# A fused layernorm + MLP on one Trainium2 core: tiles 4 to 7 transposed by DMA, tile 0 in two halves, and a reordered last group

## The chip, the cores and the metric

The kernel runs on one core of a Trainium2 chip (trn2). The time is the device time of one execution in microseconds (us). The profile's span, from the first to the last instruction, is about 2 us shorter than the time. PE is TensorE, PEld its weight loads, DVE is VectorE, ACT ScalarE, POOL GpSimd, SP SyncE (here the engine that issues nearly all DMAs).

## The reference

```python
B, S, D, F = 1, 2048, 1024, 3584          # all inputs bfloat16

def reference(x, w1, b1, w2, b2):
    y = _layernorm(x, axis=-1)             # eps 1e-5, no scale or shift
    h = gelu_tanh(einsum("bsd,df->bsf", y, w1) + b1)
    return einsum("bsf,fd->bsd", h, w2) + b2
```

## The kernel before

Both matrix products use a seven-product scheme (Strassen in Winograd's form), on sums of quarters of the operands. The sums are made on DVE. The 16 row tiles of x (128 rows each) form two blocks of 8. Each tile is normalized, and must be transposed before it can be the moving operand: `to_yT_pe` does this on PE and copies the result out of PSUM on ACT; `to_yT_dma` does it by DMA. Before, all 8 tiles of block 0 went through PE and the 8 of block 1 through DMA.

The program is not written in its final order. Each `op` and `dma` records a task with an estimated duration. A list scheduler orders the tasks of each engine, and a randomized packing places every buffer in SBUF. When two buffers share bytes, the later one's first write waits for the earlier one's last reader. So an edit anywhere moves the order and *deals the placement anew*.

The parts that the change and the argument touch:

```python
def norm(i):                              # DVE, one row tile
    for h in range(2):
        op("DVE", 0.62, ... bn_stats ...)                # statistics of half h
    op("DVE", 0.25, ... bn_aggr ...); op("DVE", 0.1, ... + eps ...)
    op("POOL", 0.5, ... pow -0.5 ...)                    # rstd
    op("DVE", 0.47, ... (x - mean) * rstd ...)           # all 1024 columns
...
def to_yT_pe(b, i, bank):                 # 8 transposes into one PSUM bank, two ACT copies out
    def f(e):
        for k in range(KD):
            r = e.transpose(out=pv[:, k, :], in_=v16(xbuf, k * 256, 256), identity=ident[:, :])
        return r
    op("PE", KD * MM128, f, ...)
    for h in range(2):
        op("ACT", A_CP, ... copy of half h ...)
...
def tsum(b, t):                           # T sums of tiles t and t + 4, on DVE
    T1 = B12 - B11;  T2 = B22 - T1;  B12 = B22 - B12 (T3);  T4 = B21 - T2
```

```python
# head: "wave" = products of 128 columns, tile by tile, 7 weight rows each
for t in range(4):
    wave(t, range(0, 4))
    if t < 3: to_yT_pe(0, t + 1, 7)
    else:     b1_transpose(7)
    wave(t, range(4, WAVE_ROWS))
...
# then full-width products (512 columns); tiles 4 to 7 are transposed among them
for r in range(RH):
    ...p1(r + 1)...; p2(r)
    if nt < 8 and r in HEAD_T:            # HEAD_T = (2, 4, 6, 7)
        to_yT_pe(0, nt, 7); tsum(0, nt - 4); nt += 1
warm(1, bank=7, full=True)
# from here on the products need T1..T4 of block 0: "the first T product" is T2's
...
flat += [(last, 7), (last, 4), (last, 3)]  # the last group's last three products
```

```python
# Wino.step, one group of seven products in four PSUM banks X, Y, Z, Wb
elif q == 7:
    self.prod(7, Y, False)
    s3 = save(Y, n + "s3", mem=MA)        # ACT copies bank Y to SBUF
    add(Z, Z, s3, n + "V")                # DVE
    self.sink["22"](Z)                    # DVE add, store
elif q == 4:
    self.prod(4, Y, False)                # adds to bank Y: waits for the copy
    self.sink["21"](Y)
```

## Time and profile before

| | before |
|---|---|
| time, median of the first 3 runs (range) | 340.43 us (340.21 to 341.08) |
| span of the profiled run | 338.0 us |
| PE busy | 331.9 us, 98% of the span, granted clock 1.00 |
| DVE busy | 295.3 us, 87% |
| first full-width product | 17.02 us |
| first T product | 32.12 us |

PE's own waits come first. Each line says who waited, for whom, and then the total in us, how often, and the longest:

```profile
PE ps L1145 <- POOL nhalf L605: 1.0, 1, 1.0
PE ps L871 <- DVE mem L751: 0.8, 1, 0.8
PE ps L1124 <- ACT mem L806: 0.7, 1, 0.7
PE ps L1175 <- ACT mem L690: 0.2, 1, 0.2
PE ps L871 <- ACT ps L797: 0.2, 1, 0.2
```

In 338 us PE shows 2.9 us of waits (the other 3.1 us without work come after its last matmul, which ends at 334.88 us). Of this, 1.0 is the start, where nothing can run yet. The 0.7 us of L1124 lies in the last group: product 4 waits for ACT's copy of bank Y.

Next is the timeline of PE in the head, in order of time. The columns are start, duration, engine, line, operation, tiles, and the count of merged instructions; in brackets stand the idle time before and what ended it:

```profile
7.35 0.62 PE L685 MATMUL ps<-ident,mem 128*128 128x128 f16 x8
...
8.65 1.07 PE L1175 MATMUL ps<-mem 128*128 128x128 f16 x16 [0.23 <-ACT mem L690]
...
10.00 1.91 PE L1175 MATMUL ps<-mem 128*128 128x128 f16 x28
...
17.02 2.75 PE L871 MATMUL ps<-mem 128*128 128x512 f16 x12
19.61 0.61 PE L685 MATMUL ps<-ident,mem 128*128 128x128 f16 x8
```

L685 are transposes and L1175 is the wave. Transposes stand between the wave's parts, and from 17.02 us on between the full-width products (L871) as well: 4 times 8 of them, 0.45 us each.

The middle, same view, from the filler product L1145 on:

```profile
31.91 0.38 PE L1145 MATMUL ps<-ones 128*128 128x512 bf16 x1
32.12 47.79 PE L871 MATMUL ps<-mem 128*128 128x512 f16 x220
...
86.39 3.84 PE L871 MATMUL ps<-mem 128*128 128x512 f16 x17 [0.82 <-DVE mem L751]
```

The first T product starts at 32.12 us. The start of the piece at 86.39 us is the 305th full-width matmul of the program. I call it **M**.

The table by stretch shows for three stretches (us) the busy time of each engine (count of instructions), the granted clock, the DMA share and the traffic:

```profile
core 0: us, PE busy (x) PEld busy (x) DVE busy (x) ACT busy (x) POOL busy (x), PEclk, DMA share, GB/s
48.00:60.00 12.00, 12.00 (x58) 5.42 (x56) 11.83 (x23) 11.49 (x22) 2.31 (x3) 1.00 1.13 338
60.00:72.00 12.00, 12.00 (x57) 5.45 (x56) 11.56 (x23) 11.88 (x23) 5.26 (x5) 1.00 1.12 345
72.00:87.00 15.00, 13.98 (x63) 5.66 (x62) 15.00 (x33) 10.23 (x18) 0.76 (x2) 1.00 1.17 301
```

PE, DVE and the DMA engines are all full here. And the traffic in the 40 slices of the span, from the page (8.45 us each):

```profile
GB/s 233 324 193 7 281 268 345 356 287 335 284 300 320 287 304 357 308 338 323 312 32 218 109 235 96 184 147 143 225 165 180 175 116 230 170 169 249 204 103 63
```

The fourth slice, from 25 to 34 us, moves next to nothing: this is the room for the DMA transposes.

The end of the kernel, timeline of all engines (weight loads and DMA issues left out):

```profile
331.01 0.58 ACT L806 COPY mem<-ps 128x512 f32<-128x512 f32 x1 [2.47 <-PE ps L1124]
...
331.65 3.23 PE L1124 MATMUL ps<-mem 128*128 128x256 f16 x28 [0.68 <-ACT mem L806]
...
333.39 0.69 DVE L1056 TENSOR_TENSOR mem<-ps,mem 128x512 bf16<-128x512 f32 x1 [0.34 <-PE ps L1124]
334.92 0.69 DVE L1056 TENSOR_TENSOR mem<-ps,mem 128x512 bf16<-128x512 f32 x1 [0.84 <-PE ps L1124]
```

L806 is the copy that product 4 waits for; the last 28 matmuls are products 4 and 3, and each then needs a 512-column finish on DVE (L1056).

### The profile page before, as it was taken

Reading aid. Unit: us, or ns where it says so; the run is one execution under the profiler, and the core shown is the slowest. Engines: PE = TensorE matmul, PEld = TensorE weight load, DVE = VectorE, ACT = ScalarE, POOL = GpSimd, SP = SyncE. Lnnn points to the kernel's source line nnn. Section 1 sums busy time; section 2 is a strip of 40 time slices with the busy share of each in tenths; the row PEclk is TensorE's granted clock in tenths of the full one; section 3 lists DMA queues with packets and bytes.
Section 4 is the critical chain, followed back from the end, with each engine's and each line's share of the span. In section 5 each row is a group of like instructions: output and inputs, shape, how many; then the busy total and the mean of one; then the engine's idle time right before and its main releaser. Section 6 shows DMA issues by size and latency. Waiting matters only on the chain.

```text
span 338.0 us, 6056 instructions
## 1 busy us (share of the span) xinstructions
PE 331.9 (98%) x2363; PEld 222.0 (66%) x2363; DVE 295.3 (87%) x481; ACT 179.4 (53%) x311; POOL 15.2 (5%) x28
## 2 busy tenths in 40 slices
PE   8999999999999999999999999999999999999995
PEld 6854444443344444444446888888888888888884
DVE  5698899999999869967978992799999999999844
ACT  2699899996667676766765545534111222222110
POOL 2210110230000000000000000000000000000000
DMA  7970899999999999999917382644756537558732
GB/s 233 324 193 7 281 268 345 356 287 335 284 300 320 287 304 357 308 338 323 312 32 218 109 235 96 184 147 143 225 165 180 175 116 230 170 169 249 204 103 63
DMA packets 99382, 75.83 MB, mean 224 GB/s; under 512 B 12186, under 2 KB 90650, under 8 KB 99354
## 3 DMA queue, kind: packets, MB, share of 16 engines
q1 hardware_dynamic: 99210, 75.32, 74.6%
q8 instruction: 18, 0.29, 0.4%
q10 hardware_dynamic: 144, 0.13, 0.1%
q14 instruction: 10, 0.08, 0.1%
HBM read 48.96 MB, written 24.38 MB: 217 GB/s over the span
## 4 chain that ended last, share of the span: by engine, by line
PE 85%; DVE 9%; DMA 2%; issue 2%; POOL 0%; ACT 0%; DVEq 0%
PE ps L1124 44%; PE ps L871 37%; DVE ps L814 2%; PE ps L1175 2%; DVE mem L751 2%; DVE mem L937 2%; DVE st_sb L656 2%; DMA mem<-in_w_dram 1%; PE ps L685 1%; DMA mem<-in_x_dram 1%; DVE mem L717 1%; POOL rstd_sb L662 0%; DVE mem L664 0%; DVE mem L1056 0%; DVE mem L651 0%
## 5 line engine op out<-in xcount | busy, mean ns | idle before, releaser
L871 PE MATMUL ps<-mem 128*128 128x512 f16 x756 | 165.4, 379 | 1.0 <-DVE mem L751 0.8
L1124 PE MATMUL ps<-mem 128*128 128x256 f16 (+1 forms) x1372 | 150.6, 273 | 0.7 <-ACT mem L806 0.7
L1124 PEld LDWEIGHTS ps<-mem 128*128 128x128 f16 x1372 | 134.1, 98 | 17.5 <-ACT mem L806 1.0
L871 PEld LDWEIGHTS ps<-mem 128*128 128x128 f16 (+1 forms) x756 | 73.2, 98 | 89.8 <-DVE mem L751 2.2
L806 ACT COPY mem<-ps 128x512 f32<-128x512 f32 x111 | 65.0, 593 | 82.3 <-PE ps L1124 67.3
L790 ACT ACTIVATE mem<-ps,b_sb 128x512 f16<-128x512 f32 x112 | 73.3, 696 | 26.1 <-PE ps L871 15.6
L814 DVE TENSOR_TENSOR ps<-ps,mem 128x512 f32<-128x512 f32 x84 | 58.3, 695 | 23.8 <-ACT mem L806 21.8
L1028 DVE TENSOR_TENSOR mem<-mem 128x1792 f16<-128x1792 f16 x56 | 59.7, 1083 | 4.2 <-PE ps L1124 4.2
L751 DVE TENSOR_TENSOR mem<-mem 128x1024 f16<-128x1024 bf16 (+1 forms) x56 | 37.5, 685 | 0.6 <-DMA mem<-in_w_dram 0.2
L937 DVE TENSOR_TENSOR mem<-mem 128x512 f16<-128x512 f16 (+5 forms) x84 | 37.4, 463 | 0.7 <-DMA mem<-in_w_dram 0.4
L1039 DVE TENSOR_TENSOR mem<-mem 128x1792 f16<-128x1792 f16 x32 | 33.4, 1084 | 0.4 <-PE ps L871 0.4
L797 ACT COPY ps<-ps 128x512 f32<-128x512 f32 x31 | 17.7, 572 | 26.5 <-PE ps L1124 20.4
L656 DVE BATCH_NORM_STATS2 st_sb<-mem 128x6 f32<-128x512 bf16 x24 | 15.6, 675 | 6.0 <-DMA mem<-in_x_dram 5.9
L1056 DVE TENSOR_TENSOR mem<-ps,mem 128x512 bf16<-128x512 f32 x24 | 16.3, 686 | 3.5 <-PE ps L1124 3.5
L921 DVE TENSOR_TENSOR mem<-mem 128x2048 f16<-128x2048 bf16 (+1 forms) x16 | 17.3, 1083 | 0.0
L1069 DVE TENSOR_TENSOR mem<-ps,mem 128x512 f32<-128x512 f32 x24 | 16.2, 682 | 0.0
L690 ACT COPY mem<-ps 128x512 f16<-128x512 f16 x16 | 8.7, 603 | 8.9 <-PE ps L685 8.9
L717 DVE TENSOR_TENSOR mem<-mem 128x512 f16<-128x512 f16 x32 | 12.2, 418 | 0.1
L662 POOL TENSOR_TENSOR rstd_sb<-vpe_sb,nhalf 128x1 f32<-128x1 f32 x12 | 7.9, 663 | 50.2 <-DVE vpe_sb L659 50.2
L1145 PE MATMUL ps<-ones 128*128 128x128 bf16 (+1 forms) x58 | 7.3, 297 | 1.0 <-POOL nhalf L605 1.0
L1175 PE MATMUL ps<-mem 128*128 128x128 f16 x112 | 7.6, 219 | 0.3 <-ACT mem L690 0.2
L664 DVE TENSOR_SCALAR mem<-mem,mv_sb,rstd_sb 128x1024 f16<-128x1024 bf16 x12 | 6.3, 536 | 0.8 <-POOL rstd_sb L662 0.7
(30 smaller groups left out, 66.5 us busy)
## 6 DMA issues: line engine op xcount, KB each, us to landing
mem<-in_w_dram SPq DMA_DIRECT2D x80, 256.0 KB, 5.0
mem<-w_scr SPq DMA_DIRECT2D x28, 448.0 KB, 3.5
w_scr<-mem SPq DMA_DIRECT2D x21, 512.0 KB, 5.2
w_raw<-mem SPq DMA_DIRECT2D x12, 512.0 KB, 5.5
mem<-w_raw SPq DMA_DIRECT2D x12, 448.0 KB, 4.3
out_dram<-mem SPq DMA_DIRECT2D x32, 128.0 KB, 2.8
mem<-in_w_dram SPq DMA_DIRECT2D x9, 448.0 KB, 4.5
mem<-in_x_dram SPq DMA_DIRECT2D x15, 256.0 KB, 4.6
```

Of the source, the lines that this page charges most:

```text
L656: op("DVE", 0.62, lambda e, i=i, h=h: e.bn_stats(st_sb[:, i, 6 * h:6 * (h + 1)], v16(b, h * D, D, BF16)), r=[b.c(h)], w=[c_st[i][h]], name ...
L751: op("DVE", d_tt(n), lambda e: e.tensor_tensor(out=o[0], in0=a[0], in1=bb[0], op=f), r=[a[1], bb[1]], w=[o[1]], name=f"w1S{k}_{ch}")
L790: op("ACT", A_GELU, lambda e: e.activation(out=dst, in_=bank2(bank), func=ACT.Gelu_apprx_tanh, bias=b1_sb[:, f:f + 1], scale=1.0), r=[bank ...
L797: op("ACT", A_CP, lambda e: e.copy(out=banks[dst][:, :], in_=banks[src][:, :]), r=[bank_c[src]], w=[bank_c[dst]], name=name, lat=A_LAT)
L806: op("ACT", A_CP, lambda e: e.copy(out=v16(a, 0, 2048, F32), in_=banks[src][:, :]), r=[bank_c[src]], w=[a.c()], name=name, lat=A_LAT)
L814: op("DVE", D_PS, lambda e: e.tensor_tensor(out=banks[dst][:, :], in0=banks[src][:, :], in1=v16(a, 0, 2048, F32), op=ALU.add), r=[bank_c[s ...
L871: i = e.matmul(banks[bank][:, :], lhsT=lv[:, k, :], rhs=rv[:, k, :], start=(fresh and k == 0), stop=(k == KH - 1), skip_group_check=True)
L921: op("DVE", d_tt(2 * self.n), lambda e: e.tensor_tensor(out=vd, in0=va, in1=vb, op=ALU.subtract), r=self.cells(a) + self.cells(bb), w=self ...
L937: tt = lambda o, a, c: (lambda e: e.tensor_tensor(out=o, in0=a, in1=c, op=ALU.subtract))
L1028: op("DVE", d_tt(UN // 2), lambda e: e.tensor_tensor(out=v16(t), in0=a[0], in1=bb[0], op=f), r=a[1] + bb[1], w=[t.c()], name=f"in{b}_{p}{q}")
L1039: op("DVE", d_tt(UN // 2), lambda e, va=va, vb=vb, vd=vd: e.tensor_tensor(out=vd, in0=va, in1=vb, op=f), r=h_cells(b, a, u, s) + h_cells(b ...
L1124: i = e.matmul(bank2(bank)[:, t, :], lhsT=av3[:, k, t * P:(t + 1) * P], rhs=bv[:, k, :], start=(fresh and t == 0 and k == 0), stop=(t == 1 ...
```

## The change

The intent is to take work out of PE's stream at three places. At the head, PE shall start earlier, on half a normalized tile, and the seven weight rows of each wave tile stand 3 + 4 around the next tile's transposes instead of 4 + 3. In the middle, DMA shall transpose tiles 4 to 7, in a time when it is idle. At the end, product 3 shall hide the copy that product 4 waits for, and product 4 shall come in two halves in two fresh banks, so that the finish of the first overlaps the second. The rest tunes the scheduler to this: a look-ahead of 0.3 us (HOLD), another assumed start of PE, another packing seed, and more lead for the w2 units.

```diff
+HOLD = 0.3
-HEAD_T = (2, 4, 6, 7)
-UNIT_LA, IN_LA = (4, 5), 5
+UNIT_LA, IN_LA = (6, 5), 5
-T_PE = 7.5
-SEED = 2
+T_PE = 6.0
+SEED = 6
+HEAD_DUE = (6.0, 2.0)
...   scheduler: an engine may wait up to HOLD for a more urgent task; packing: more starts
-                op("DVE", 0.47, lambda e: e.tensor_scalar(out=v16(b), ...
+                for o, n in ((0, D * 2),) if i else ((0, D), (D, D)):
+                    op("DVE", 0.47 if i else 0.27, lambda e, o=o, n=n: e.tensor_scalar(
...
-            to_yT_pe(0, 0, 7)
-            warm(8, bank=6)
+            to_yT_pe(0, 0, 7, 6)          # half 0 into bank 7, half 1 into bank 6
+            warm(5, bank=5)
...
-                wave(t, range(0, 4))
+                wave(t, range(0, 3))
...
-                wave(t, range(4, WAVE_ROWS))
+                wave(t, range(3, WAVE_ROWS))
...
-            nt = 4
+            for i in range(4, 8):
+                due(lambda: (to_yT_dma(0, i), tsum(0, i - 4)), HEAD_DUE[0] + HEAD_DUE[1] * (i - 4))()
             for r in range(RH):
...
-                if nt < 8 and r in HEAD_T:
-                    to_yT_pe(0, nt, 7)
-                    tsum(0, nt - 4)
-                    nt += 1
...
-            flat += [(last, 7), (last, 4), (last, 3)]
+            flat += [(last, 7), (last, 3), (last, 4)]
...
+                    elif q == 4 and self.last:
+                        self.sink["21"](Y, (self.prod, self.s3, (X, (X + 4) % 8)))
...
+                        elif p == 3 and end is not None:
+                            prod, s3, fresh = end
+                            e6 = E.pop(("6", k))
+                            op("DVE", D_PS, ... e6 += s3 ...)
+                            for t in range(2):
+                                prod(4, fresh[t], True, t)
+                                finish(b, 0, 1, u, v, banks[fresh[t]][:, :], ..., t, 1, ("ACTQ", "SP")[t])
```

More of the change, by code (lines that the diff above doesn't have):

```diff
@@ L200, in pack @@
         weight = {i: self.size[i] * (self.gone[i] - self.born[i]) for i in ids}
-        order = sorted(ids, key=lambda i: -weight[i])
-        for tries in range(400):
+        for tries in range(600):
+            if tries % 100 == 0:
+                order = sorted(ids, key=lambda i: -weight[i] * (rng.uniform(0.7, 1.3) if tries else 1.0))
             self.off[:] = -1
@@ L385, in _simulate @@
                             break
-                        _, _, t = heapq.heappop(heaps[e])
+                        t = heaps[e][0][2]
+                        if HOLD and any(r < now + HOLD and w.alap < min(t.alap - 0.05, now + 4.0) and r < now + t.dur for r, _, w in waiting[e]):
+                            break
+                        heapq.heappop(heaps[e])
                     t.start = now
@@ L663, in norm @@
                    r=[c_vpe[i], c_nh], w=[c_rstd[i]], name=f"rstd{i}", lat=0.2)
-                op("DVE", 0.47, lambda e: e.tensor_scalar(out=v16(b), in0=v16(b, 0, D * 2, BF16), scalar1=mv_sb[:, i, 0:1],
-                                                          scalar2=rstd_sb[:, i:i + 1], op0=ALU.subtract, op1=ALU.mult),
-                   r=[c_mv[i], c_rstd[i]], w=[b.c(0), b.c(1)], name=f"norm{i}")
+                for o, n in ((0, D * 2),) if i else ((0, D), (D, D)):
+                    op("DVE", 0.47 if i else 0.27, lambda e, o=o, n=n: e.tensor_scalar(
+                        out=v16(b, o, n), in0=v16(b, o, n, BF16), scalar1=mv_sb[:, i, 0:1], scalar2=rstd_sb[:, i:i + 1],
+                        op0=ALU.subtract, op1=ALU.mult),
+                       r=[c_mv[i], c_rstd[i]], w=[b.c(h) for h in range(2) if o <= h * D < o + n], name=f"norm{i}")
             y = {}
@@ L675, in yv, with to_yT_pe, tr, f @@
                 return v3(y[b, c], 0, KD * CT * 2, KD)
-            def to_yT_pe(b, i, bank):
+            def to_yT_pe(b, i, bank, other=None):
                 c, t = (i % 8) // 4, i % 4
                 xbuf = xb[i]
-                pv = banks[bank][:, :].bitcast(F16).rearrange("p (k s) -> p k s", k=KD)
-                def f(e):
-                    for k in range(KD):
-                        r = e.transpose(out=pv[:, k, :], in_=v16(xbuf, k * 256, 256), identity=ident[:, :])
-                    return r
-                op("PE", KD * MM128, f, r=[xbuf.c(0), xbuf.c(1), c_id], w=[bank_c[bank]], name=f"T{i}", lat=PE_LAT)
+                pv = [banks[z][:, :].bitcast(F16).rearrange("p (k s) -> p k s", k=KD) for z in (bank, bank if other is None else other)]
+                cell = [bank_c[bank], bank_c[bank if other is None else other]]
+                def tr(ks):
+                    def f(e):
+                        for k in ks:
+                            r = e.transpose(out=pv[k // KH][:, k, :], in_=v16(xbuf, k * 256, 256), identity=ident[:, :])
+                        return r
+                    return f
+                if other is None:
+                    op("PE", KD * MM128, tr(range(KD)), r=[xbuf.c(0), xbuf.c(1), c_id], w=[cell[0]], name=f"T{i}", lat=PE_LAT)
+                else:
+                    for h in range(2):
+                        op("PE", KH * MM128, tr(range(h * KH, (h + 1) * KH)), r=[xbuf.c(h), c_id], w=[cell[h]], name=f"T{i}_{h}", lat=PE_LAT)
                 yy = yv(b, c)
@@ L690, in to_yT_pe @@
                     op("ACT", A_CP, lambda e, h=h: e.copy(out=yy[:, h * KH:(h + 1) * KH, t * P:(t + 1) * P],
-                                                         in_=pv[:, h * KH:(h + 1) * KH, :]),
-                       r=[bank_c[bank]], w=[y[b, c].c((h, t))], name=f"Te{i}_{h}", lat=A_LAT)
+                                                         in_=pv[h][:, h * KH:(h + 1) * KH, :]),
+                       r=[cell[h]], w=[y[b, c].c((h, t))], name=f"Te{i}_{h}", lat=A_LAT)
                 M.free(xbuf)
@@ L822, in __init__ @@
                     self.X, self.Y, self.Z, self.Wb = (4 * bset + k for k in range(4))
-                    self.s1 = None
+                    self.s1, self.last = None, False
                     self.done = set()
@@ L856, in step @@
                         add(Z, Z, s3, n + "V")
-                        MA.free(s3)
+                        if self.last:
+                            self.s3 = s3
+                        else:
+                            MA.free(s3)
                         self.sink["22"](Z)
+                    elif q == 4 and self.last:
+                        self.sink["21"](Y, (self.prod, self.s3, (X, (X + 4) % 8)))
+                        MA.free(self.s3)
                     elif q == 4:
@@ L1043, in out_sum, with store, finish @@
                         H[b, nm, s] = H.pop((b, place, s))
-            def store(b, i, k, u, v, o):
-                tb = b * TB + i * 512 + u * 256
+            def store(b, i, k, u, v, o, t0=0, nt=2, q="SP"):
+                tb = b * TB + i * 512 + u * 256 + t0 * P
                 c0 = k * 512 + v * NCOL
-                dma("SP", lambda e: e.dma_start(of[tb:tb + 256, c0:c0 + NCOL].rearrange("(t p) c -> p t c", p=P),
-                                                v16(o, 0, 1024, BF16).rearrange("p (t c) -> p t c", t=2)),
-                    [o.c()], [], P * 1024, None, f"st{b}{i}{k}{u}{v}")
+                dma(q, lambda e: e.dma_start(of[tb:tb + nt * P, c0:c0 + NCOL].rearrange("(t p) c -> p t c", p=P),
+                                                v16(o, 0, nt * 512, BF16).rearrange("p (t c) -> p t c", t=nt)),
+                    [o.c()], [], P * nt * 512, None, f"st{b}{i}{k}{u}{v}")
                 M.free(o)
-            def finish(b, i, k, u, v, a, na, bb, nb, name):
-                o = M.alloc(1024, "o")
-                op("DVE", D_PS, lambda e: e.tensor_tensor(out=v16(o, 0, 1024, BF16), in0=a, in1=bb, op=ALU.add),
+            def finish(b, i, k, u, v, a, na, bb, nb, name, t0=0, nt=2, q="SP"):
+                o = M.alloc(nt * 512, "o")
+                n = nt * NCOL
+                a, bb = a[:, t0 * NCOL:t0 * NCOL + n], bb[:, t0 * NCOL:t0 * NCOL + n]
+                op("DVE", 0.08 + n / 960, lambda e: e.tensor_tensor(out=v16(o, 0, 2 * n, BF16), in0=a, in1=bb, op=ALU.add),
                    r=[na, nb], w=[o.c()], name=name, lat=D_PS_LAT)
-                store(b, i, k, u, v, o)
+                store(b, i, k, u, v, o, t0, nt, q)
             E = {}
@@ L1070, in addto, with f @@
                            r=[bank_c[bank], src.c()], w=[dst.c()], name=name, lat=D_PS_LAT)
-                    def f(bank):
+                    def f(bank, end=None):
                         k = (b, u, v)
@@ L1095, in f @@
                             addto(e6, bank, e6, n)
+                        elif p == 3 and end is not None:
+                            prod, s3, fresh = end
+                            e6 = E.pop(("6", k))
+                            op("DVE", D_PS, lambda e: e.tensor_tensor(out=av(e6), in0=av(e6), in1=av(s3), op=ALU.add),
+                               r=[e6.c(), s3.c()], w=[e6.c()], name=n + "s3", lat=D_PS_LAT)
+                            for t in range(2):
+                                prod(4, fresh[t], True, t)
+                                finish(b, 0, 1, u, v, banks[fresh[t]][:, :], bank_c[fresh[t]], av(e6), e6.c(), f"{n}_{t}", t, 1,
+                                       ("ACTQ", "SP")[t])
+                            M.free(e6)
                         elif p == 3:
                             e6 = E.pop(("6", k))
-                            finish(b, 0, 1, u, v, banks[bank][:, :], bank_c[bank], av(e6), e6.c(), n)
+                            finish(b, 0, 1, u, v, banks[bank][:, :], bank_c[bank], av(e6), e6.c(), n, q="ACTQ" if (b, u) == (NB - 1, 1) else "SP")
                             M.free(e6)
@@ L1114, in prod2, with f @@
             def prod2(b, p):
-                def f(q, bank, fresh):
+                def f(q, bank, fresh, t=None):
                     av_, ac = a_unit(b, p, q)
@@ L1119, in f @@
                     bf = UNITS[p, q]
+                    ts = range(2) if t is None else (t,)
                     def g(e):
-                        for t in range(2):
+                        for t in ts:
                             for k in range(KQ):
                                 i = e.matmul(bank2(bank)[:, t, :], lhsT=av3[:, k, t * P:(t + 1) * P], rhs=bv[:, k, :],
-                                             start=(fresh and t == 0 and k == 0), stop=(t == 1 and k == KQ - 1), skip_group_check=True)
+                                             start=(fresh and t == ts[0] and k == 0), stop=(t == ts[-1] and k == KQ - 1), skip_group_check=True)
                         return i
-                    op("PE", 2 * KQ * MM256, g, r=ac + [bf.c()] + ([] if fresh else [bank_c[bank]]), w=[bank_c[bank]],
+                    op("PE", len(ts) * KQ * MM256, g, r=ac + [bf.c()] + ([] if fresh else [bank_c[bank]]), w=[bank_c[bank]],
                        name=f"m2_{b}_{p}{q}", lat=PE_LAT)
-                    if b == NB - 1:
-                        M.free(UNITS.pop((p, q)))
-                    ina_drop(b, p, q)
+                    if t != 0:
+                        if b == NB - 1:
+                            M.free(UNITS.pop((p, q)))
+                        ina_drop(b, p, q)
                 return f
@@ L1147, in warm, with due, g @@
                 op("PE", n * (MM512 if full else MM128), f, r=[c_ones] + ([gate] if gate is not None else []), w=[bank_c[bank]], name="warm")
+            def due(f, after):
+                def g():
+                    pr.due = (pr.last_pe, after)
+                    f()
+                    pr.due = None
+                return g
             y_new(0, 0)
@@ L1220, in build @@
                 p2(r)
-                if nt < 8 and r in HEAD_T:
-                    to_yT_pe(0, nt, 7)
-                    tsum(0, nt - 4)
-                    nt += 1
-            assert nt == 8
             warm(1, bank=7, full=True)
@@ L1277, in build @@
             fC = first_use(c_seq[0], (1,))
-            def due(f, after):
-                def g():
-                    pr.due = (pr.last_pe, after)
-                    f()
-                    pr.due = None
-                return g
             y1at = Y1_AT
@@ L1351, in build @@
                 n_g += 1
-            import os
+            groups[last].last = True
             for i, (g, q) in enumerate(flat):
```

## The prediction

> **What bounds the kernel.** TensorE. The page has PE busy 331.9 of 338.0 us at full clock, and the chain of waits is 85% PE. PE's own wait list is short: 1.0 us at the start, 0.7 before the last 28 matmuls (on the ACT copy L806), 0.8 at 85.6 us (on DVE's weight sum L751), 0.2 and 0.2. VectorE is a close second: the windows show it busy 11.8 of 12, 11.6 of 12 and 15.0 of 15 us between 48 and 87 us, and the chain runs through it from 52.6 to 86.4 us. Only work taken out of PE's stream, or out of the ends, counts, and DVE may take it back.
>
> **What changes, costed from the trace.**
> 1. *Head.* Before, the norm of tile 0 starts at 6.75, its 8 transposes at 7.35, the ACT copy at 8.01, the first wave matmul at 8.65. With halves the first transposes need half a norm (about 0.28 instead of 0.48 us), and only 4 transposes (0.22 of 0.45 us) come before the copy. The order shows one more statistics instruction ahead, costing about 0.1 us. Gain about 0.4 us. Weights (landing 6.8, 7.7, 8.5, 10.1 us) and x tile 3 (9.3 us) are just early enough.
> 2. *Middle.* Four PE transposes at 0.45 us leave: 1.8 us. With the head, PE would want the first T product at about 30.0 instead of 32.3 us. But the four DMA transposes are issued behind the weight loads, from about 20.4 us on, at 1.2 to 2.6 us each, and landed 2.5 to 3.5 us after issue in the trace; tile 7 should land at 29 to 30 us. DMA was idle here (7 GB/s in the fourth slice). The Trainium skill, "Advanced Engine Details and Errata", section X-Bar Transpose, says such transposes are as fast as regular DMAs; the trace agrees on packets alone (1024 of 256 bytes in 1.0 us when queued behind others, 2.4 us when not), not on issue. DVE is tighter still: from 20.7 us it has two norms, six weight sums (0.6 us pitch) and fourteen T sums (0.335) until the last tile's T2, ready at about 30.7. So PE will probably wait 0.5 to 1 us before the first T product. Net about 1.0 us.
> 3. *DVE-bound stretch to 87 us.* The order shows nearly the same DVE work ahead of each chunk's sums; its idle 2.4 us around 33 to 36 us shrinks, so the shift passes on. The waits of 1.0 us at 80 and 86 us change by some tenths at most.
> 4. *Tail.* Product 3 now stands between 7 and 4, and 4 goes into fresh banks: the 0.68 us PE wait goes. One more DVE add (about 0.6 us) comes in; the last add is 256 instead of 512 wide (about 0.4 of 0.69 us). DVE ends the kernel: V add, s3 add, two full finishes, two halves, done about 3.9 us after product 7, against 4.6 before. The last store (1.84 us to landing) hardly shortens. Gain about 0.7 us.
>
> **Sum.** About 0.4 + 1.0 + 0.2 + 0.7 = 2.3 us: **338.0 us**, range 336.3 to 339.6. Faster by over 2% (below 333.6) 2%, within 2% 97%, slower 1%.
>
> **What would show it.** First wave matmul at 8.2 to 8.3; no transposes in PE after tile 3; a PE wait before the first T product at 29.8 to 31 us, put down to DVE T sums or a transposing DMA; PE busy about 330; no gap before the last 28 matmuls; DVE back to back at the end.
>
> **What would make it wrong.** Transposes landing after 31 us (a stall eats the 1.8 us); landing before 28 with DVE ahead (gain to 3.5 us); new waits on weight units or buffers from the other packing; DVE falling behind between 48 and 87 us.

## The result, and the profile after

| | before | after |
|---|---|---|
| time, median (range) of 4 runs each | 340.32 us (339.98 to 341.08) | 338.19 us (337.74 to 338.62) |
| span of the profiled run | 338.0 us | 336.0 us |
| PE busy | 331.9 us | 329.9 us |
| DVE busy | 295.3 us | 298.3 us |

The ratio is 0.9934, with a 95% interval of 0.9910 to 0.9958: faster by 0.4 to 0.9%, clear of noise, but small. Ratios here and below are the mean time of one kernel's runs over that of the other's of the same rounds, so not quite the ratio of the medians that I quote.

PE's waits after:

```profile
PE ps L1180 <- POOL nhalf L610: 1.0, 1, 1.0
PE ps L891 <- DVE mem L731: 0.8, 1, 0.8
PE ps L891 <- ACT ps L811: 0.4, 1, 0.4
PE ps L891 <- DVE mem L765: 0.4, 1, 0.4
PE ps L1217 <- DMA mem<-in_w_dram: 0.2, 1, 0.2
PE ps L891 <- ACT mem L804: 0.2, 1, 0.2
```

The wait in the last group (0.7 us on ACT) is gone. New is 0.8 us on DVE L731: that line is the T sums.

PE in the head (L1217 is the wave, L891 the full-width products):

```profile
8.57 0.84 PE L1217 MATMUL ps<-mem 128*128 128x128 f16 x12
...
9.70 0.83 PE L1217 MATMUL ps<-mem 128*128 128x128 f16 x12
10.74 1.05 PE L1217 MATMUL ps<-mem 128*128 128x128 f16 x16 [0.20 <-DMA mem<-in_w_dram]
...
12.07 1.73 PE L1217 MATMUL ps<-mem 128*128 128x128 f16 x28
...
16.76 13.11 PE L891 MATMUL ps<-mem 128*128 128x512 f16 x60
...
30.87 5.35 PE L891 MATMUL ps<-mem 128*128 128x512 f16 x24 [0.78 <-DVE mem L731]
```

The first wave matmul starts at 8.57 us, only 0.08 us earlier than before. DVE's norm of tile 0 tells why. Before (L664, whole) and after (L670, two halves):

```profile
6.75 0.55 DVE L664 TENSOR_SCALAR mem<-mem,mv_sb,rstd_sb 128x1024 f16<-128x1024 bf16 x1
7.04 0.72 DVE L670 TENSOR_SCALAR mem<-mem,mv_sb,rstd_sb 128x512 f16<-128x512 bf16 x2
```

From there to the first wave matmul it takes 1.53 us instead of 1.90, but the norm starts 0.29 us later. On the other hand, 28 wave matmuls now take 1.73 us instead of 1.91. At 10.74 us PE waits 0.20 us for the weights of the wave's last row. The full-width products start at 16.76 instead of 17.02 us, and run through without transposes. The first T product comes at 30.87 us, after 0.78 us of waiting. The transposes on SP's queue, and the T sums on DVE in the same time, are these:

```profile
20.04 7.05 SPq L713 DMA_TRANSPOSE mem<-mem  x4
```

```profile
25.53 5.95 DVE L731 TENSOR_TENSOR mem<-mem 128x512 f16<-128x512 f16 x16 [0.16 <-DMA mem<-mem]
31.40 1.41 DVE L765 TENSOR_TENSOR mem<-mem 128x1024 f16<-128x1024 f16 x2
```

The trace has the four transposes landing at 25.50, 26.35, 27.76 and 28.96 us. The 16 T sums then run back to back. The 14th, T2 of the last pair of tiles, ends at 30.81 us, and PE goes on at 30.87 us.

The rest of PE's waits, and the same stretches as before:

```profile
75.84 2.76 PE L891 MATMUL ps<-mem 128*128 128x512 f16 x12 [0.42 <-DVE mem L765]
78.78 6.34 PE L891 MATMUL ps<-mem 128*128 128x512 f16 x28 [0.17 <-ACT mem L804]
85.54 4.71 PE L891 MATMUL ps<-mem 128*128 128x512 f16 x21 [0.42 <-ACT ps L811]
```

```profile
48.00:60.00 12.00, 12.00 (x57) 5.38 (x56) 11.45 (x22) 11.40 (x21) 1.92 (x3) 1.00 1.17 315
60.00:72.00 12.00, 11.97 (x56) 5.25 (x55) 11.93 (x24) 11.87 (x22) 2.49 (x3) 1.00 1.05 322
72.00:87.00 15.00, 13.99 (x63) 5.55 (x61) 14.86 (x34) 10.69 (x19) 1.67 (x3) 1.00 1.15 296
```

M is at 85.54 us. The end:

```profile
329.28 3.77 PE L1158 MATMUL ps<-mem 128*128 128x256 f16 x33
...
330.02 0.58 ACT L820 COPY mem<-ps 128x512 f32<-128x512 f32 x1 [2.47 <-PE ps L1158]
330.64 0.70 DVE L828 TENSOR_TENSOR ps<-ps,mem 128x512 f32<-128x512 f32 x1 [1.46 <-ACT mem L820]
331.25 0.68 DVE L1121 TENSOR_TENSOR mem<-mem 128x512 f32<-128x512 f32 x1
331.85 1.94 DVE L1078 TENSOR_TENSOR mem<-ps,mem 128x512 bf16<-128x512 f32 x4
```

PE runs through all the last products (L1158, 33 in the piece) and DVE ends the kernel: V add, the new add of s3 (L1121), two full finishes and two halves in one piece (L1078 x4).

The span's 1.96 us divide by PE's marks as follows. In each trace all 756 full-width matmuls and all 1372 of the output stage are recorded.

| stretch | before | after | gain, us |
|---|---|---|---|
| start to first full-width product | 17.02 | 16.76 | 0.26 |
| to the first T product | 15.10 | 14.11 | 0.99 |
| to the first output-stage matmul (181.49, 180.51 us) | 149.37 | 149.64 | -0.27 |
| to the end of the span | 156.47 | 155.49 | 0.98 |

### The profile page after: what moved, and what is told of

Read it like the earlier page. It is cut to its first block, busy times and chain, and to the rows that moved or that the text cites. A ratio compares the mean times of both kernels' runs of the same rounds, so it can differ in the third digit from the quotient of the medians.

```text
span 336.0 us, 6016 instructions
## 1 busy us (share of the span) xinstructions
PE 329.9 (98%) x2328; PEld 220.3 (66%) x2328; DVE 298.3 (89%) x484; ACT 178.7 (53%) x303; POOL 13.4 (4%) x28
## 4 chain that ended last, share of the span: by engine, by line
PE 88%; issue 3%; ACT 3%; DMA 2%; DVE 1%; SPq 1%; POOL 0%; POOLq 0%; DVEq 0%
PE ps L1158 44%; PE ps L891 43%; DMA mem<-in_w_dram 2%; PE ps L1217 2%; ACT mem L820 1%; ACT mem L804 1%; SPq L754 0%; DVE mem L1078 0%; SPq L637 0%; DVE mem L731 0%; ACT mem L644 0%; ACT mem L647 0%; ACT ps L856 0%; PE ps L694 0%; DVE ps L828 0%
## 5 line engine op out<-in xcount | busy, mean ns | idle before, releaser
L891 PE MATMUL ps<-mem 128*128 128x512 f16 x756 | 165.0, 379 | 1.8 <-DVE mem L731 0.8
L1158 PE MATMUL ps<-mem 128*128 128x256 f16 (+1 forms) x1372 | 150.4, 273 | 0.0
L1158 PEld LDWEIGHTS ps<-mem 128*128 128x128 f16 x1372 | 134.2, 98 | 16.4
L891 PEld LDWEIGHTS ps<-mem 128*128 128x128 f16 (+1 forms) x756 | 73.1, 98 | 92.1 <-DVE mem L765 2.5
L804 ACT ACTIVATE mem<-ps,b_sb 128x512 f16<-128x512 f32 x112 | 74.6, 691 | 23.0 <-DVE ps L828 12.2
L661 DVE BATCH_NORM_STATS2 st_sb<-mem 128x6 f32<-128x512 bf16 x24 | 15.5, 675 | 4.0 <-DMA mem<-in_x_dram 4.0
L1078 DVE TENSOR_TENSOR mem<-ps,mem 128x512 bf16<-128x512 f32 (+1 forms) x25 | 16.2, 664 | 2.7 <-PE ps L1158 2.6
L731 DVE TENSOR_TENSOR mem<-mem 128x512 f16<-128x512 f16 x32 | 12.1, 419 | 0.3 <-DMA mem<-mem 0.2
L704 ACT COPY mem<-ps 128x512 f16<-128x512 f16 x8 | 4.3, 588 | 8.6 <-PE ps L694 8.6
L1217 PE MATMUL ps<-mem 128*128 128x128 f16 x112 | 7.2, 219 | 0.3 <-DMA mem<-in_w_dram 0.2
L670 DVE TENSOR_SCALAR mem<-mem,mv_sb,rstd_sb 128x1024 f16<-128x1024 bf16 (+1 forms) x13 | 6.7, 520 | 0.5 <-POOL rstd_sb L667 0.3
```

The source lines that it names most:

```text
L804: op("ACT", A_GELU, lambda e: e.activation(out=dst, in_=bank2(bank), func=ACT.Gelu_apprx_tanh, bias=b1_sb[:, f:f + 1], scale=1.0), r=[bank ...
L891: i = e.matmul(banks[bank][:, :], lhsT=lv[:, k, :], rhs=rv[:, k, :], start=(fresh and k == 0), stop=(k == KH - 1), skip_group_check=True)
L1078: op("DVE", 0.08 + n / 960, lambda e: e.tensor_tensor(out=v16(o, 0, 2 * n, BF16), in0=a, in1=bb, op=ALU.add), r=[na, nb], w=[o.c()], name= ...
L1158: i = e.matmul(bank2(bank)[:, t, :], lhsT=av3[:, k, t * P:(t + 1) * P], rhs=bv[:, k, :], start=(fresh and t == ts[0] and k == 0), stop=(t ...
```

## The experiments

Twelve runs were made, two of them repetitions. Unless told otherwise each is the changed kernel with one edit. Nearly every edit also re-deals the placement, and this costs or gains something of its own, so I read each effect at the place where the edit acts, from the trace. The table has the marks of all traces in us. "Over pace" is the time from the first T product to M, less 52.76 us; that is what these 244 matmuls take at the pace of the changed kernel's chain of waits, which has a piece of 440 such matmuls in 95.14 us.

| kernel | first full-width product | first T product | M | over pace | first output-stage matmul | span |
|---|---|---|---|---|---|---|
| before | 17.02 | 32.12 | 86.39 | 1.51 | 181.49 | 337.96 |
| changed | 16.76 | 30.87 | 85.54 | 1.91 | 180.51 | 336.00 |
| changed_again | 16.48 | 30.66 | 85.63 | 2.21 | 181.07 | 336.56 |
| whole_tile0 | 16.75 | 30.68 | 85.60 | 2.16 | 181.17 | 336.63 |
| rows4 | 17.23 | 30.41 | 85.41 | 2.24 | 182.66 | 338.13 |
| pe_transposes | 16.63 | 31.58 | 85.65 | 1.31 | 181.05 | 337.19 |
| sched_tail | 17.18 | 32.13 | 87.06 | 2.17 | 182.03 | 337.48 |
| t12_first | 16.77 | 30.03 | 85.59 | 2.80 | 186.31 | 341.76 |
| t12_fixed | 16.68 | 29.84 | 83.94 | 1.34 | 179.38 | 334.86 |
| t12_fixed_again | 16.39 | 29.96 | 84.50 | 1.78 | 179.50 | 334.99 |
| stats_light | 16.75 | 30.44 | 85.12 | 1.92 | 181.44 | 336.92 |
| stats_light_t12 | 16.63 | 30.70 | 85.99 | 2.53 | 181.76 | 337.26 |
| old_tail | 16.81 | 30.64 | 85.37 | 1.97 | 180.94 | 337.39 |
| one_bank | 16.55 | 30.27 | 84.62 | 1.59 | 180.07 | 335.72 |

The timed runs resolve about 0.25%, that is 0.8 us. One and the same program had the ratios 0.9934 and 0.9913 to the kernel before. Times are given, but differences of some tenths rest on the traces, one execution each. No run changed the packing seed alone, so how much of the 2.1 us between the two kernels is a luckier deal of the placement is not shown.

### whole_tile0: tile 0 whole again

```diff
-                for o, n in ((0, D * 2),) if i else ((0, D), (D, D)):
+                for o, n in ((0, D * 2),):
...
-            to_yT_pe(0, 0, 7, 6)
+            to_yT_pe(0, 0, 7)
```

> The changed kernel with tile 0 normalized and transposed whole again (one norm, eight transposes into one bank, the rest as changed). Theory A (the head is bounded by the landing of the weights for wave row 6, 10.6 us in the changed kernel's trace, not by the norm): first wave matmul about 0.3 us later (8.9 instead of 8.57 us), but the start of the full-width products (16.76 us) moves by at most 0.15 us and the time by less than 0.2 us. Rival B (the halves gave the head's gain): the start of the full-width products moves by 0.3 to 0.4 us, and the first T product with it unless DVE's T sums are later anyway.

Measured: 338.39 us (before in the same rounds 341.05), ratio 0.9914 (0.9894 to 0.9934). The first wave matmul moved to 8.92 us. The full-width products started at 16.75 us, the same as with halves (16.76), although PE waited 0.20 us for weights in the trace with halves and not in this one. The nine other traces that have halves and the 3 + 4 split start them between 16.39 and 16.81 us. These marks move with DVE's first statistics, which started between 3.36 and 3.83 us, so it is better to count from points within each trace. From the start of the norm to the first wave matmul it took 1.53 us in all eleven traces with halves, and 1.89 us here: the halves save 0.36 us. From the first statistics to the full-width products it took 12.98 to 13.18 us in these nine traces, and 13.34 us both here and in the changed kernel's trace, which lost the 0.36 us again to late weights. In the changed kernel nothing is left of it at the first T product, where PE waits. The part of theory A about weights is only half shown: they took the gain in that trace, not in the others.

### rows4: the wave split 4 + 3 again, halves kept

```diff
-                wave(t, range(0, 3))
+                wave(t, range(0, 4))
...
-                wave(t, range(3, WAVE_ROWS))
+                wave(t, range(4, WAVE_ROWS))
```

> The changed kernel with the wave split 4 + 3 around the transposes again, halves kept. Theory A (the split 3 + 4 gave the head's gain, since four rows, 0.9 us, cover the copy of the next tile out of PSUM and three rows, 0.67 us, do not): the weight loads wait for the copies again, about 0.2 us at each of three tiles, and the start of the full-width products moves from 16.76 to about 17.1 us or later. Rival B (the halves gave it): it stays within 0.15 us of 16.76. The time moves little in either case if the first T product waits for DVE anyway (A and B alike: under 0.3 us).

Measured: 340.38 us (before 341.05), ratio 0.9981 (0.9960 to 1.0001). The full-width products started at 17.23 us. PE's timeline has the reason, the 28 wave matmuls between two transposes at the old 1.91 us:

```profile
10.21 1.91 PE L1217 MATMUL ps<-mem 128*128 128x128 f16 x28
...
17.23 1.03 PE L891 MATMUL ps<-mem 128*128 128x512 f16 x4
```

So theory A is right about the split: from the first wave matmul to the full-width products it took 8.37 us in the three traces with 4 + 3 (before, rows4, sched_tail) and 7.82 to 8.19 us in the eleven with 3 + 4. With four rows after the transposes, PE has work for as long as ACT copies the transposed tile out of PSUM; with three it waits about 0.18 us at each tile. Yet the first T product came at 30.41 us, no later than in the changed kernel. PE reached it here without a wait, 13.18 us after the first full-width product (14.11 in the changed kernel, with its wait): the later head only used up the time that the changed kernel waits. The time is longer than the changed kernel's because of a 1.05 us wait of PE at 165.38 us (on ACT), and other small ones, that the changed kernel's trace does not have. I put this down to the re-dealt placement, which the pair t12_first and t12_fixed tests below; for rows4 itself that is not tested.

### pe_transposes: tiles 4 to 7 on PE again

```diff
-            for i in range(4, 8):
-                due(lambda: (to_yT_dma(0, i), tsum(0, i - 4)), HEAD_DUE[0] + HEAD_DUE[1] * (i - 4))()
+            nt = 4
...
+                if nt < 8 and r in (2, 4, 6, 7):
+                    to_yT_pe(0, nt, 7)
+                    tsum(0, nt - 4)
+                    nt += 1
```

> The changed kernel with tiles 4 to 7 transposed on TensorE again. Theory A (the DMA transposes take 1.8 us out of PE's stream, of which the wait for the T sums gives 0.8 back): first T product at about 31.7 us instead of 30.87 with no wait before it, PE busy about 1.8 us more, time 0.5 to 0.9 us longer than the changed kernel. Rival B (VectorE between 48 and 87 us decides, so an earlier start is given back): first T product later by the same 0.9, but product 304 (85.5 us in the changed kernel) within 0.2 us and the time within 0.3 us of the changed kernel.

Measured: 339.40 us (before 341.05), ratio 0.9950 (0.9930 to 0.9971). The first T product came at 31.58 us with no wait before it. This is 0.7 us later than in the changed kernel (30.87), 0.9 later than in changed_again (30.66), and 0.54 us earlier than before (32.12): without a wait on T sums the head's gain does reach it. So in the changed kernel the DMA transposes bring 0.7 to 0.9 of the 1.8 us that they take out of PE's stream, as far as the first T product. But M was at 85.65 us, where rival B had put it, and the first output-stage matmul at 181.05 us, against 180.51 and 181.07 in the two traces of the changed kernel. So this run does not show that the gain reaches the end. Its longer span comes in good part from the output stage (156.13 us), where PE waited 0.33 us for weights, at a place that the edit does not touch.

### t12_first: T1 and T2 of all tiles ahead of T3 and T4

```diff
-                due(lambda: (to_yT_dma(0, i), tsum(0, i - 4)), HEAD_DUE[0] + HEAD_DUE[1] * (i - 4))()
+                due(lambda: (to_yT_dma(0, i), tsum(0, i - 4, (0,))), HEAD_DUE[0] + HEAD_DUE[1] * (i - 4))()
+            for i in range(4, 8):
+                due(lambda: tsum(0, i - 4, (1,)), 14.0)()
...   tsum: T1 and T2 if 0 in part, T3 and T4 if 1 in part
```

> The changed kernel with the T sums of block 0 reordered on VectorE: T1 and T2 of all four tiles first, then T3 and T4. Both theories: T2 of the last tile is ready about 0.8 us after the last transposing DMA lands (28.96 us) instead of 30.81, so the first T product starts at about 29.9 to 30.1 us and PE's 0.78 us wait there goes. Theory A (the shift passes on to the end): time 0.6 to 0.8 us shorter than the changed kernel, about 337.4 us. Rival B (VectorE, busy throughout from 48 to 87 us, takes it back as waits of PE for weight sums): product 304 stays at about 85.5 us, PE waits between 60 and 87 us grow from 1.0 to about 1.8 us, time within 0.2 us.

Measured: 343.36 us (before 341.05), ratio 1.0063 (1.0035 to 1.0090), slower than the kernel before. The first T product came at 30.03 us as expected, and M at 85.59 us as B says. What nobody expected is this line of PE's timeline:

```profile
162.16 8.12 PE L893 MATMUL ps<-mem 128*128 128x512 f16 x29 [3.60 <-DVE mem L767]
```

PE waited 3.60 us for a weight sum (L767), some 130 us after the edited place. This also cost clock. The table by stretch for 158 to 166 us:

```profile
158.00:166.00 8.00, 4.41 (x14) 1.56 (x13) 6.64 (x16) 2.27 (x4) 0.00 (x0) 0.80 0.95 287
```

The granted clock was 0.80 on average there (1.00 up to 162 us, 0.50 from 163 to 166), and 0.995 over the span, where nearly all other profiled runs had 1.000 (stats_light 0.999). The Trainium skill, "TensorE: Matmul & The Clock Gate", Part 1, says that an idle window of about 3.4 us brings the clock down to half; this trace agrees, with 0.50 after 3.60 us of idle. Either the reorder did this, or the placement that was dealt with it.

### t12_fixed: the same reorder, the placement of the changed kernel kept

The placement is computed from the unedited program, and only the final program has the edit; the sequence of buffers is the same, so the placement is valid.

```diff
+        NEW = [False]
...
-                due(lambda: (to_yT_dma(0, i), tsum(0, i - 4)), HEAD_DUE[0] + HEAD_DUE[1] * (i - 4))()
+                due(lambda: (to_yT_dma(0, i), tsum(0, i - 4, (0,) if NEW[0] else (0, 1))), HEAD_DUE[0] + HEAD_DUE[1] * (i - 4))()
+            for i in range(4, 8) if NEW[0] else ():
+                due(lambda: tsum(0, i - 4, (1,)), 14.0)()
...
+        NEW[0] = False
         first = Program()
...
+            NEW[0] = True
             got, placed = Program(), Placed(plan)
```

> The T sums reordered as in t12_first, but with the buffers placed exactly where the changed kernel has them (the placement is computed from the unedited program; only the final program has the edit). Theory B (VectorE's stretch up to 86 us decides; the 3.6 us gap at 162 us in t12_first came from the other placement): first T product at about 30.0 us, product 304 again at 85.4 to 85.7 us, no gap over 1 us near 162 us, time within 0.3 us of the changed kernel (338.2). Theory A (the shift passes on): product 304 at about 84.8, time 337.4 us. Theory C (the reorder itself caused the loss): the gap near 162 us and a time of 342 to 343 us again.

Measured: 338.41 us (336.62 to 339.66; before 341.22), ratio 0.9921 (0.9894 to 0.9949), and a span of 334.86 us in the profile. PE goes from the filler straight into the first T product:

```profile
29.63 0.38 PE L1184 MATMUL ps<-ones 128*128 128x512 bf16 x1
29.84 6.36 PE L895 MATMUL ps<-mem 128*128 128x512 f16 x28
```

M came at 83.94 us, and no wait longer than 0.5 us is left on PE after the start-up. So theory C is out: the loss of t12_first came with the placement dealt anew, and not from the reorder alone. B's number for M (85.4 to 85.7) is wrong too: here the shift passed on, and more than that. But the timed runs scatter over 3 us, and the profiled execution is the fastest of the six (336.62 us, median 338.41).

### sched_tail: head and middle undone, scheduler settings and tail kept

```diff
-SEED = 6
+SEED = 7
-                for o, n in ((0, D * 2),) if i else ((0, D), (D, D)):
+                for o, n in ((0, D * 2),):
-            to_yT_pe(0, 0, 7, 6)
-            warm(5, bank=5)
+            to_yT_pe(0, 0, 7)
+            warm(8, bank=6)
...   wave(t, range(0, 4)) / wave(t, range(4, WAVE_ROWS)); tiles 4 to 7 as in pe_transposes
```

> The changed kernel with all its head and middle edits undone: tile 0 whole, wave split 4 + 3, tiles 4 to 7 transposed on TensorE. Kept: the tail and the scheduler's settings (look-ahead, time offset, unit lead; seed 7, since the placement is dealt anew). Theory B (only the scheduler's order up to 86 us and the tail gain anything): first T product at 32.0 to 32.3 us as before, product 304 at 85.5 to 85.8 instead of 86.39, tail 1.0 us shorter, time within 0.5 us of the changed kernel unless the new placement leaves a wait after 87 us, which the trace would show. Theory A (the head and the middle carried 1.3 us): product 304 at 86.4 or later, time about 339.4 us.

Measured: 339.40 us (before 341.22), ratio 0.9951 (0.9931 to 0.9971). The first T product came at 32.13 us, as before (32.12), and M at 87.06 us. Theory B, by which the scheduler's settings alone give the changed kernel's M, is refuted. Over pace it lost 2.17 us, more than the kernel before. The output stage took 155.45 us, so the tail's gain is all there.

### stats_light: 3.7 us of VectorE's work taken away

```diff
-  e.bn_stats(st_sb[:, i, 6 * h:6 * (h + 1)], v16(b, h * D, D, BF16))
+  e.bn_stats(st_sb[:, i, 6 * h:6 * (h + 1)], v16(b, h * D, 128 if i >= 8 else D, BF16))
```

> The changed kernel, but the 8 statistics instructions of tiles 9, 11, 13 and 15 on VectorE read 64 of their 512 columns (result wrong on purpose; same instructions, order, placement). It takes about 3.6 us (8 times 0.45) of VectorE's time away before 86 us and nothing from TensorE. Theory B (VectorE's work decides when PE passes product 304): product 304 moves from 85.54 to between 83.6 (PE's own pace, 244 times 0.216 us from 30.87) and 84.5 us, and the time falls by 1 to 2 us. Theory A (PE's stream decides there): product 304 stays within 0.3 us of 85.5.

Measured: 339.18 us (before 341.22), ratio 0.9954 (0.9920 to 0.9989). The result is wrong, though it still passed the comparison, whose tolerance is evidently wider than this. Up to M the 24 statistics instructions took 11.8 us instead of 15.5 (changed). M moved to 85.12 us, 0.42 earlier, and this is the 0.43 us by which the first T product came earlier: over pace it lost 1.92 us, as the changed kernel (1.91). DVE's freed time turned into idle time:

```profile
48.00:60.00 12.00, 12.00 (x57) 5.38 (x56) 10.04 (x19) 10.90 (x21) 1.75 (x3) 1.00 1.16 286
60.00:72.00 12.00, 11.70 (x54) 4.97 (x53) 10.87 (x24) 11.87 (x22) 2.55 (x3) 1.00 1.08 308
72.00:87.00 15.00, 14.14 (x65) 5.84 (x63) 13.15 (x32) 10.65 (x19) 1.93 (x3) 1.00 1.14 307
```

Compare the last three lines of this view of the changed kernel: DVE was busy 11.45, 11.93 and 14.86 us there, and 10.04, 10.87 and 13.15 here, with the same 12, 12 and 15 us to be filled. So DVE is full in the changed kernel there, and still 3.7 us less work hardly moved M. In this trace DVE's own longest waits from 20 to 90 us were for weights by DMA (2.4 us) and for transposing DMAs (1.9 us). One caution: the weights requested at 62 to 63 us landed at 67.5 and 68.3 us here and at 65.9 and 66.7 us in the changed kernel. changed_again below had them at 67.3 and 68.1 us and lost 2.21 us, so with like landings the lighter DVE gained 0.29 us. PE's longest wait in the stretch (0.68 us at 76.13 us) was still for a weight sum of DVE. What is shown is that DVE's load alone does not decide; that late weights do is argued. Past M this run lost another 1.3 us (96.32 us from M to the output stage, 94.97 in the changed kernel), so its time says little.

### stats_light_t12: both together

The two edits of stats_light and t12_fixed.

> stats_light with the T sums in the order of t12_fixed, placement as in the changed kernel (result wrong on purpose). Theory B: with VectorE relieved, the earlier first T product (30.0 instead of 30.87) is no longer taken back: product 304 comes 0.5 to 0.9 us earlier than in stats_light. If the shift is taken back again although VectorE is relieved (within 0.2 us of stats_light), something other than VectorE's load holds PE there.

Measured: 338.78 us (before 341.22), ratio 0.9932 (0.9903 to 0.9961). It decides nothing. The premise failed, since the last of the four transposes landed only at 29.64 us (28.33 and 28.90 in the two runs of t12_fixed), and the first T product came at 30.70 us instead of 30.0. M was at 85.99 us: with DVE relieved, PE lost 2.53 us over pace, where t12_fixed lost 1.34 and 1.78. The weights for the chunk that was requested at 62 to 63 us landed at 68.4 and 69.2 us here, and at 65.6 and 66.4 in both runs of t12_fixed. Late landings and time lost go together in these three traces; no run changed the landings alone.

### changed_again and t12_fixed_again, side by side

Both are unedited repetitions on one chip, in the same rounds.

> The changed kernel, unedited, once more, beside t12_fixed_again on the same chip. It tells how far times and the places of the trace's marks move between runs of one program: first T product within 0.4 us of 30.87 (it follows the landing of the first transposing DMA), ratio to the kernel before 0.991 to 0.996, as on record (0.9934).

> t12_fixed, unedited, once more, on the same chip as changed_again. If the first T product's 0.8 to 1.0 us pass on to the end (as the first trace of t12_fixed showed: span 334.9 against 336.0 us), it is 0.7 to 1.2 us faster than changed_again in the medians of the same rounds, and no PE wait near 31 us. If that trace was luck, the two agree within 0.4 us.

Measured: changed_again 338.21 us (337.24 to 339.12), ratio 0.9913 (0.9883 to 0.9942); t12_fixed_again 337.27 us (336.72 to 338.50), ratio 0.9892 (0.9865 to 0.9919); before 341.33 us. The first T product came at 30.66 and 29.96 us, and the spans of the two traces are 336.56 and 334.99 us. In the medians the reorder wins 0.94 us over the changed kernel, in the two pairs of traces 1.1 and 1.6 us. The intervals of the two ratios overlap, so the timed runs alone do not settle it. Both traces of t12_fixed are of the fastest execution, while changed_again's is near its median, so the traces favour it. Its two spans are the shortest of all traces; but that the whole shift passes on is likely, not shown. The wait at the first T product was not quite zero this time (0.24 us), since the last transpose landed at 28.90 us.

### old_tail: the tail of the kernel before

```diff
-            flat += [(last, 7), (last, 3), (last, 4)]
+            flat += [(last, 7), (last, 4), (last, 3)]
...
-            groups[last].last = True
-  finish(..., n, q="ACTQ" if (b, u) == (NB - 1, 1) else "SP")
+  finish(..., n)
```

> The changed kernel with the tail of the kernel before (products 7, 4, 3; one finish of 512 columns each; no store from ACT). Only the stretch from the first w2 product on counts for it, since the placement is dealt anew: PE's 0.68 us wait before the last 28 matmuls is back, and the stretch from the first w2 product to the end of the span takes about 156.5 us, as before, instead of 155.5. Rival (the tail's gain comes from the stores or from other waits in the output stage): the stretch stays within 0.3 us of 155.5 although the wait is back.

Measured: 339.08 us (before 341.33), ratio 0.9936 (0.9909 to 0.9963). The wait is back, at the same 0.68 us:

```profile
331.09 3.23 PE L1158 MATMUL ps<-mem 128*128 128x256 f16 x28 [0.68 <-ACT mem L820]
```

From the first output-stage matmul to the end of the span it took 156.45 us, against 156.47 before and 155.49 in both traces of the changed kernel. The tail's gain, 0.96 us, is the most repeatable number: the ten traces with the new tail, these two included, took 155.45 to 155.50 us. The one exception is pe_transposes (156.13), with the wait for weights told above and a last store that landed 0.15 us later.

### one_bank: product 4 whole, in one fresh bank

```diff
-                            for t in range(2):
-                                prod(4, fresh[t], True, t)
-                                finish(b, 0, 1, u, v, banks[fresh[t]][:, :], ..., f"{n}_{t}", t, 1, ("ACTQ", "SP")[t])
+                            prod(4, fresh[0], True)
+                            finish(b, 0, 1, u, v, banks[fresh[0]][:, :], bank_c[fresh[0]], av(e6), e6.c(), n)
```

> The changed kernel, but the last product 4 goes whole into one fresh bank and is finished by one add of 512 columns and one store (seed 5, placement dealt anew). Theory A (the reorder, which lets product 3 hide the copy, makes the tail's gain; the two banks hardly matter, since VectorE is still busy with the earlier adds when the first half is ready): from the start of the last 28 matmuls to the end of the span 6.1 to 6.4 us, against 6.18 in the changed kernel and 6.31 before; PE without a wait before them. Rival B (the two banks carry a third of the gain or more): 6.5 us or longer.

Measured: 337.62 us (before 341.33), ratio 0.9896 (0.9867 to 0.9926). There was no wait before the last 28 matmuls, and from their start to the end of the span it took 6.34 us, against 6.18 in the changed kernel and 6.31 before. The stretch of the output stage took 155.65 us. So of the 0.98 us the reorder with a fresh bank gives 0.82, and the two banks with their halves 0.16 at most: pe_transposes, which has the two banks, took 6.33 us too. Theory A holds.

## Why the prediction was right

Time and range were right: 338.0 us predicted, 338.19 measured. By terms, with the gain of the traces beside it:

1. *Head: 0.4 predicted, 0.26 measured, and from other parts.* The prediction credited the halves, and expected the first wave matmul at 8.2 to 8.3 us. It came at 8.57. The halves did save 0.37 us (1.53 instead of 1.90 us from the norm to the first wave matmul; 0.43 by the prediction's own figures). But the order put one more statistics instruction, an aggregate and a small add of tile 1 ahead of the norm, and this cost 0.35 us (3.63 instead of 3.28 us from the first statistics to the norm), not "about 0.1". What remained came from the split of the wave, 3 + 4 instead of 4 + 3, which the prediction passed over: it is worth 0.55 us (rows4), of which late weights took 0.36 in this trace; the prediction had called the weights "just early enough". In the changed kernel the wait on T sums then hides the head altogether.
2. *Middle: 1.0 predicted, 0.99 measured.* The parts were right as well: the last transpose landed at 28.96 us (predicted 29 to 30), T2 ended at 30.81 (30.7), PE waited 0.78 us (0.5 to 1) and the wait was put down to DVE's T sums. t12_fixed shows the cause by removing it: with T1 and T2 first, the wait goes. All this holds up to the first T product. Whether the 1.0 us reaches the end is open: pe_transposes shows 0 to 0.5 us at the output stage, while in the traces of t12_fixed a further shift did pass on.
3. *Stretch to 87 us: 0.2 gain predicted, 0.27 loss measured up to the output stage.* That "the shift passes on" was right on the whole. The first T product came 1.25 us earlier and the first output-stage matmul still 0.98 us earlier. The waits that PE's list shows there kept their sum (0.19 + 0.82 us before, 0.42 + 0.17 + 0.42 after), as said, but the time over pace rose from 1.51 to 1.91 us. The start times of the matmuls show where: in the changed kernel six matmuls came late, by 0.19, 0.14, 0.58, 0.34, 0.11 and 0.58 us (at 64.7, 74.4, 75.8, 78.8, 82.4 and 85.5 us), and all others kept the pace. The list leaves out up to 0.16 us of each such delay and does not show the small ones at all: a record of a 512-column matmul is 0.38 us long, while in an undisturbed stretch such matmuls start every 0.216 us. That DVE is "a close second" limit was read from its occupancy, and stats_light speaks against it: 3.7 us less work on DVE left the time over pace at 1.92 us (1.91 and 2.21 in the two traces of the changed kernel). Why these matmuls come late, 1.3 to 2.8 us in all 14 traces, was not settled. It differs by up to 0.44 us between two runs of one program and by 1 to 1.5 us between placements of one edit; late weight landings go with it in part (not in the pair of t12_fixed, whose 0.44 us stands at the start, at 32.3 us, while its weights landed alike).
4. *Tail: 0.7 predicted, 0.98 measured.* The wait went as said; it was listed as 0.68 us, but by the start times it was worth 0.84, for the same reason as in the stretch. The prediction counted from the end of product 7 to the end of DVE's work, 4.6 to 3.9 us. Measured were 4.60 (from 331.01 to 335.61 us) and 3.77 us (330.02 to 333.79). The last store, which it took as unchanged, landed 1.69 us after its issue instead of 1.84.

So two misses, in the head and in the stretch, were partly made up by a tail that came out larger: 2.3 us in the sum, 1.96 in the traces, 2.13 in the medians. That the total came within 0.2 us is in part luck. The middle, the one term with a real argument behind a partial gain, was right up to the first T product.

## What to carry to other kernels

When work leaves a busy engine, look for the next thing that the following step needs: here 1.8 us of transposes left PE, and the wait for VectorE's sums took 0.8 back, until the sums that are needed first were put first. Where a scheduler and a packing sit between the source and the program, an edit also deals the cards anew: hold the placement fixed, or read the effect where the edit acts, before you believe a total. An engine that is full is not yet the one that decides: take some of its work away and look.

## What the Trainium skill lacked or had wrong

- "Advanced Engine Details and Errata", X-Bar Transpose, expects 350 to 400 GB/s and transposes as fast as regular DMAs. Four transposes of 256 KB, issued one behind the other from SP, landed 1.15 us apart on average (25.50 to 28.96 us), 227 GB/s. But each took SP 1.3 to 2.7 us to issue, and the last three landed 1.9 to 2.1 us after their issue had ended, so SP's issue set this pace and the page's rate was not tested. What the section lacks is the issue cost.
- "VectorE: DVE Perf Modes", The three transpose paths, gives 390 ns on TensorE and 1309 ns by DMA for 128x128. Back to back, 8 transposes on PE added 0.45 us to the chain (56 ns each), and by DMA 1.15 us per 8 (144 ns each). That section has no sustained rates.
- "Perfetto Trace Analysis", Identifying the Most-Contended Engine, takes occupancy as the measure for VectorE and says to optimize the engine with the highest first. Here VectorE was busy 38.24 of 39 us (48 to 87 us), and with 3.7 us taken away the time that PE lost there hardly fell (1.92 us, against 1.91 and 2.21 in the two traces of the changed kernel). What the same section says of matmul busy time agrees: from the first T product to M the changed kernel lost 1.91 us, of which PE's idle time shows 0.42 + 0.17 + 0.42.
- No page speaks of the repeatability of DMA under full load: loads of one program, requested at the same place, landed up to 1.4 us apart in two runs (65.9 and 67.3 us in the changed kernel).
